# A linear-attention and Mish block on one core: column pieces of the first weights, an interleaved seam between two stages, and two transposes moved

## Chip, core and metric

The kernel runs on one core of a Trainium2 chip. The metric is the device time of one execution in microseconds (us).

The engines are called as the profile calls them: PE is TensorE's matmuls, PEld its weight loads, DVE is VectorE, ACT is ScalarE, POOL is GpSimd, SP issues transfers. Each operation passes through one helper line of the source (L62), so rows are told apart by their tiles, not by their line.

Some words that come back: a *bank* is one of the eight PSUM buffers into which the program lets its matmuls write; to *evacuate* a bank is to copy it out with DVE or ACT, after which it can be used again. A *group* is the eight matmuls that add up in one bank. `rstd` is the factor of a layer norm, which POOL computes; `xr` is the copy of x that is loaded a second time for the residual sum; `KVZ` holds the products kv and z. The *granted clock* is the share of full speed that the profile records for TensorE.

## The reference, cut to what matters

```python
x = A_x                                     # 1 x 2048 x 1024, bf16
h  = x + A(layernorm(x), wqkv, wo)          # linear attention, 32 heads of 32
h2 = h + B(layernorm(h), w1, b1, w2)        # F = 3584

# A: phi(t) = where(t > 0, t + 1, exp(t)) + 1e-6
kv  = sum over s of phi(k) v ;  z = sum over s of phi(k)
o   = phi(q) kv / (phi(q) z + 1e-6) ;  A = o @ wo
# B: u = x @ w1 + b1 ;  act = u * tanh(softplus(u)) ;  B = act @ w2
```

The rows are handled in 16 tiles of 128. TensorE is busy for 668.4 us of the span, the next engine, ACT, for 338.8, so what can be won is TensorE's idle time, and its time at a reduced clock.

## The kernel before: the parts concerned

The program is written as five queues of operations, one for each engine, with explicit semaphore waits; an engine executes its queue in order (in the trace of before, an ACT copy whose input is ready at 326.40 us starts at 340.31, when the ACT work queued ahead of it is done). `ins` adds an operation and returns a token, `wait` makes the queue wait for one.

*The start.* The K and V columns of wqkv arrive in four pieces by rows. The first group of eight matmuls (k = 0 to 7) accumulates over all 1024 rows, so it needs all four pieces:

```python
T_b1 = sp.dma(b1row[:, :], b1_v, d_b1)
T_wkv = [pool.dma(wqkv_sb[:, 2*i:2*i+2, D:3*D], wqkv_v[:, 2*i:2*i+2, D:3*D], d_wkv[i]) for i in range(4)]
T_wq = pool.dma(...) ; T_wo = pool.dma(...)
# b1: a PE transpose and a DVE copy, first in both queues        (cut)
for t in range(NT):
    ...                                       # transposes(t + 1), LN1_prep(t + 2)
    for j in range(4):
        for k in range(KT):
            if t == 0 and j == 0 and k % 2 == 0:
                pe.wait(T_wkv[k // 2])
            tk = pe.ins("matmul", bank[:, :], lhsT=xnT[:, k, ...], rhs=wqkv_sb[:, k, D + j*512: ...], ...)
    if t % 4 == 3:                            # after every fourth tile: 8 groups of Q, on two PSUM banks
        ...
```

*The seam.* After the last Q block come eight groups of KV products, each copied out of PSUM by eight small DVE copies, and only then the first attention tile:

```python
for g in range(NG):
    ...                                       # 16 matmuls into bank g % 4
    for j in range(4):
        dve.ins("tensor_copy", KVZ[rs, g, 32*j:32*(j+1)], bank[rs, 32*j:32*(j+1)], mark=False)
        tkz = dve.ins("tensor_copy", KVZ[rs, g, 128+j:129+j], bank[rs, 128:129])
def stage_A(t):
    pe.wait(T_KVZ[NG - 1])
    ...
for i in range(NT + 1):                       # A: numerator, denominator; B: transpose; C: wo, residual; D: transpose
    stage_A(i); stage_B(i - 1); stage_C(i - 2); stage_D(i - 3)          # bounds of i cut
```

*The tail of that loop.* The transposes of the last two tiles (D) stand behind the first chunk of the second half. Both write the same PSUM bank, and the second waits for the ACT copy of the first:

```python
def stage_D(t):
    pe.wait(T_hn[t])
    if t >= 1:
        pe.wait(T_hnT[t - 1])                 # the one bank must be empty
    tb = tpview(hn_bank)
    ...                                       # 8 transposes
    act.wait(tk_)
    T_hnT[t] = act.ins("activation", hnT[...], tb[:, :, :], ACT.Copy)

H_chunk(0)                                    # layernorm(h) @ w1 for 256 rows; on ACT: Exp, Ln, Tanh in batches
stage_D(NT - 2)
stage_D(NT - 1)
H_chunk(1)
I_chunk(0)                                    # act @ w2
```

Of the kernel before, what the change touches and what calls it, by code (L numbers as in the profile page):

```python
# [20 lines left out]
class _Q:  # L21
# [24 lines left out]
            self.waited[tok.key] = tok.val  # L46
            self.ops.append(("w", tok.sem, tok.val))

    def dma(self, out, in_, dsem, inc=16, **kwargs):
        dsem.total += inc  # L50
        self.ops.append(("d", out, in_, dsem.sem, inc, kwargs))
        return _Tok(dsem.sem, dsem.total, dsem.key)

    def emit(self, block):
        ops = self.ops

        def section(eng):
            for op in ops:
                k = op[0]
                if k == "i":  # L60
                    _, method, args, kwargs, sem = op
                    i = getattr(eng, method)(*args, **kwargs)  # L62
                    if sem is not None:
                        i.then_inc(sem, 1)
                elif k == "w":
                    eng.wait_ge(op[1], op[2])
                else:
                    _, out, in_, sem, inc, kwargs = op
                    eng.dma_start(out, in_, **kwargs).then_inc(sem, inc)

        getattr(block, self.kind)(section)

# [11 lines left out]
def bass_sequential_preLN__linear_attn_block__dense_activation_mish__prompt_kernel(  # L84
# [4 lines left out]
    NT = S // 128  # L89
# [105 lines left out]
    T_x = {}  # L195
    for t in range(min(NXS, NT)):
        T_x[t] = sp.dma(xs[:, t % NXS, :], x_t[t], d_x[t % NXS])
    T_b1 = sp.dma(b1row[:, :], b1_v, d_b1)
    T_wkv = [pool.dma(wqkv_sb[:, 2 * i:2 * i + 2, D:3 * D], wqkv_v[:, 2 * i:2 * i + 2, D:3 * D], d_wkv[i])
             for i in range(4)]  # L200
    T_wq = pool.dma(wqkv_sb[:, :, 0:D], wqkv_v[:, :, 0:D], d_wq)
    T_wo = pool.dma(wo_sb[:, :, :], wo_v, d_wo)

    pe.wait(T_ident, T_b1)
    t_b1 = pe.ins("transpose", tpview(banks[0])[:, 0, 0:FT], b1row[:, :], ident[0:FT, 0:FT])
    dve.wait(t_b1)
    T_b1col = dve.ins("tensor_copy", b1col[:, :], tpview(banks[0])[:, 0, 0:FT])

    T_tp = {}
    T_tpev = {}  # L210
# [41 lines left out]

    def transposes(u):
        tb = tpview(banks[u % 2])
        pe.wait(T_norm[u])
        if u == 0:
            pe.wait(T_b1col)
        if u >= 2:
            pe.wait(T_tpev[u - 2])
        for k in range(KT):  # L260
# [6 lines left out]
    q_banks = [banks[6], banks[7]]  # L267
    q_use = [0]
    T_qbank_free = [None, None]

    LN1_prep(0)
    if NT > 1:
        LN1_prep(1)
    transposes(0)

    for t in range(NT):
        if t + 1 < NT:
            transposes(t + 1)
        if t + 2 < NT:
            LN1_prep(t + 2)  # L280
        pe.wait(T_tpev[t])
        for j in range(4):
            bank = kv_banks[j]
            if t >= 1:
                pe.wait(T_kvev[(t - 1, j)])
            for k in range(KT):
                if t == 0 and j == 0 and k % 2 == 0:
                    pe.wait(T_wkv[k // 2])
                tk = pe.ins("matmul", bank[:, :], lhsT=xnT[:, k, t * 128:(t + 1) * 128],
                            rhs=wqkv_sb[:, k, D + j * 512:D + (j + 1) * 512], start=(k == 0), stop=(k == KT - 1),  # L290
                            mark=(k == KT - 1))
            if j < 2:
                act.wait(tk)
                dve.wait(tk)
                td = phi_evac(bank, pk[:, t, j * 512:(j + 1) * 512])
                T_kvev[(t, j)] = td
                T_pk[t] = td
            else:
                act.wait(tk)
                gs = 4 * (j - 2)  # L300
                T_kvev[(t, j)] = act.ins("activation", v_ext[:, t, gs:gs + 4, 0:128],
                                         bank[:, :].rearrange("p (g c) -> p g c", g=4), ACT.Copy)
                T_v[t] = T_kvev[(t, j)]
        if t % 4 == 3:
            c = t // 4
            pe.wait(T_wq)
            for g in range(NG):
                qb = q_use[0] % 2
                q_use[0] += 1
                bank = q_banks[qb]  # L310
                pe.wait(T_qbank_free[qb])
                for k in range(KT):
                    tk = pe.ins("matmul", bank[:, :], lhsT=wqkv_sb[:, k, g * 128:(g + 1) * 128],
                                rhs=xnT[:, k, c * 512:(c + 1) * 512], start=(k == 0), stop=(k == KT - 1),
                                mark=(k == KT - 1))
                act.wait(tk)
                dve.wait(tk)
                td = phi_evac(bank, pqT[:, g, c * 512:(c + 1) * 512])
                T_qbank_free[qb] = td
                T_qev[(g, c)] = td  # L320

    T_phase1_pe = tk

    if dbg is not None and "pk" in dbg:
        sp.wait(T_pk[NT - 1], T_v[NT - 1], T_qev[(NG - 1, NT // 4 - 1)])
        for t in range(NT):
            sp.dma(dbg["pk"][t], pk[:, t, :], d_dbg)
            sp.dma(dbg["v"][t], v_ext[:, t, :, 0:128], d_dbg)
        for g in range(NG):
            sp.dma(dbg["pqT"][g], pqT[:, g, :], d_dbg)  # L330
        for k in range(KT):
            sp.dma(dbg["xnT"][k], xnT[:, k, :], d_dbg)

    kvb = [banks[2], banks[3], banks[4], banks[5]]
    T_KVZ = {}
    for g in range(NG):
        bank = kvb[g % 4]
        if g < 4:
            pe.wait(T_kvev[(NT - 1, g)])
        else:  # L340
            pe.wait(T_KVZ[g - 4])
        pe.wait(T_pk[NT - 1], T_v[NT - 1])
        for t in range(NT):
            tk = pe.ins("matmul", bank[:, 0:129], lhsT=pk[:, t, g * 128:(g + 1) * 128], rhs=v_ext[:, t, g, 0:129],
                        start=(t == 0), stop=(t == NT - 1), mark=(t == NT - 1))
        dve.wait(tk, T_const)
        for j in range(4):
            rs = slice(32 * j, 32 * (j + 1))
            dve.ins("tensor_copy", KVZ[rs, g, 32 * j:32 * (j + 1)], bank[rs, 32 * j:32 * (j + 1)], mark=False)
            tkz = dve.ins("tensor_copy", KVZ[rs, g, 128 + j:129 + j], bank[rs, 128:129])  # L350
        T_KVZ[g] = tkz

    if dbg is not None and "KVZ" in dbg:
        sp.wait(T_KVZ[NG - 1])
        sp.dma(dbg["KVZ"], KVZ[:, :, :], d_dbg)

    act.wait(T_phase1_pe, T_tpev[NT - 1], T_norm[NT - 1])
    T_w1 = [act.dma(w1_sb[:, 4 * i:4 * i + 4, :], w1_v[:, 4 * i:4 * i + 4, :], d_w1[i]) for i in range(2)]

    if stop_after == "phase2":  # L360
        _finish(nc, sp, act, pe, dve, pool, [d_dbg] if dbg is not None else [])
        return

    att_banks = [banks[4], banks[5], banks[6]]
    otp_bank = banks[7]
    h_banks = [banks[0], banks[1]]
    hn_bank = banks[2]
    T_attev = {}
    T_oT = {}
    T_otp = {}  # L370
# [5 lines left out]
    T_xr = {}  # L376
    T_hstore = {}

    sp.wait(T_KVZ[NG - 1])
    for t in range(3):  # L380
        T_xr[t] = sp.dma(xr[:, t % 3, :], x_t[t], d_xr[t % 3])

    def stage_A(t):
        ob = t % 2
# [47 lines left out]
    def stage_C(t):  # L432
        ob = t % 2
        hs = t % 3
        pe.wait(T_oT[t], T_wo, T_xr[t])
        if t >= 1:
            pe.wait(T_hev[t - 1])
        htok = []
# [33 lines left out]
        T_hn[t] = dve.ins("tensor_scalar", hn[:, ob, :], hst[:, hs, :], mv[:, r, 0:1], rstd[:, r:r + 1],  # L472
                          op0=ALU.subtract, op1=ALU.mult)

    def stage_D(t):
        ob = t % 2
        pe.wait(T_hn[t])
        if t >= 1:
            pe.wait(T_hnT[t - 1])
        tb = tpview(hn_bank)  # L480
        for k in range(KT):
            tk_ = pe.ins("transpose", tb[:, k, :], hn[:, ob, k * 128:(k + 1) * 128], ident[:, :], mark=(k == KT - 1))
        T_hntp[t] = tk_
        act.wait(tk_)
        T_hnT[t] = act.ins("activation", hnT[:, t // 2, :, (t % 2) * 128:(t % 2) * 128 + 128], tb[:, :, :], ACT.Copy)

    for i in range(NT + 1):
        if i < NT:
            stage_A(i)
        if 0 <= i - 1 < NT:  # L490
            stage_B(i - 1)
        if 0 <= i - 2 < NT:
            stage_C(i - 2)
        if 0 <= i - 3 < NT:
            stage_D(i - 3)
# [40 lines left out]

    pool.wait(d_hst[0].tok(), d_hst[1].tok(), d_hst[2].tok())
    sp.wait(T_hev[NT - 1])
    dve.wait(T_wol[NT - 1])

    def H_chunk(c):
        ab = c % 2
        MBPc = MBP_list[c]
        pe.wait(T_w1[0], T_w1[1], T_b1col, T_attev[NT - 1])
        pe.wait(T_hnT[2 * c], T_hnT[2 * c + 1])
        if c >= 2:
            pe.wait(T_f2done[c - 2])
# [4 lines left out]
        while p0 < NPR:  # L552
# [3 lines left out]
            for p in batch:  # L556
                ent = hb_fifo.pop(0)
                prent[p] = ent
                for e_ in range(2):
# [13 lines left out]
                                 op0=ALU.add)  # L573
                    T_f1free[fb] = th
                hbtok[p] = th
            wks = {}
            te = {}
            for p in batch:
# [10 lines left out]
            for p in batch:  # L589
                act.wait(tl[p])  # L590
                tt[p] = act.ins("activation", wk_ring[:, wks[p], :, :], wk_ring[:, wks[p], :, :], ACT.Tanh)
            for p in batch:
                pool.wait(tt[p], hbtok[p])
                if c >= 2:
# [50 lines left out]
            sp.wait(tko)  # L645
            T_ost[t] = sp.dma(out_t[t], ost[:, t % 2, :], d_ost[t % 2])

    H_chunk(0)
    if not tail_D_done[0]:
        stage_D(NT - 2)  # L650
        stage_D(NT - 1)
    H_chunk(1)
    I_chunk(0)
    for c in range(2, NCH):
# [42 lines left out]
```

## Time and profile before

| | before |
|---|---|
| time, median of the first 5 runs | 715.23 us (714.94 to 717.22) |
| span of the profiled run | 713.6 us |
| PE busy | 668.4 us (94%) |
| mean granted TensorE clock | 0.978 |

A page of a profile is read from the top down: busy shares first, then the span in 40 slices, then the waits. Two more lines of the windows view give the measure that the change is held to. Columns: stretch, length, busy time (and instructions) of PE, PEld, DVE, ACT and POOL, granted clock, share of the DMA engines, GB/s.

```profile
180.20:217.34 37.14, 29.68 (x242) 18.18 (x241) 23.76 (x101) 7.42 (x11) 0.00 (x0) 0.86 0.55 219
299.70:393.09 93.39, 76.88 (x578) 56.92 (x576) 31.15 (x65) 61.53 (x97) 31.89 (x29) 0.91 0.26 91
```

The first runs from the last Q block to the second half of the first output projection, the second from chunk 0 to chunk 2 of the second half. PE is idle for 7.5 us in the one and 16.5 us in the other, at a granted clock of 0.86 and 0.91.

### The profile page before, as it was taken

The numbers are of one execution on the slowest core, as the hardware profiler recorded it, in microseconds if no ns is written. First come the engines' busy times: TensorE is split into PE (matmuls) and PEld (weight loads), VectorE is DVE, ScalarE is ACT, GpSimd is POOL, SyncE is SP. The second block draws the span as 40 slices with busy tenths as digits, with TensorE's granted clock in tenths as the row PEclk, the third lists the DMA queues.
The fourth block names the chain that finished last, engine by engine and source line by source line (L and its number), as shares of the span: only waits on it lengthen the run. The fifth ranks groups of instructions, "written<-read, shape, count | busy, mean of one in ns | idle before, by whom it ended". The sixth has DMA issues, their size and how long they took to land.

```text
span 713.6 us, 10800 instructions
## 1 busy us (share of the span) xinstructions
PE 668.4 (94%) x4385; PEld 404.5 (57%) x4385; DVE 319.1 (45%) x737; ACT 338.8 (47%) x533; POOL 150.0 (21%) x162
## 2 busy tenths in 40 slices
PE   2999999999969999992899999999999999999998
PEld 1444434444455555582774865856847748658443
DVE  4556647564486788651331522513514315225111
ACT  0233333333304555469493592681862934916800
POOL 4000000000000100106144062061350440531600
PEclk9999999999979999997799999999999999999999
DMA  8610101100093322290000001001001010010001
GB/s 308 252 30 16 31 15 30 31 1 0 1 401 118 117 89 89 87 382 20 1 16 30 30 1 60 1 28 32 2 30 30 2 29 30 1 60 1 31 30 44
DMA packets 18428, 44.74 MB, mean 63 GB/s; under 512 B 1482, under 2 KB 1482, under 8 KB 18378
## 3 DMA queue, kind: packets, MB, share of 16 engines
q1 hardware_dynamic: 11562, 20.98, 9.2%
q10 hardware_dynamic: 4672, 14.68, 5.4%
q0 software_dynamic: 2144, 8.39, 3.1%
q8 instruction: 34, 0.56, 0.3%
q14 instruction: 16, 0.13, 0.1%
HBM read 35.66 MB, written 8.39 MB: 62 GB/s over the span
## 4 chain that ended last, share of the span: by engine, by line
PE 81%; DVE 9%; ACT 6%; DMA 2%; POOL 1%; issue 1%; DVEq 0%; POOLq 0%
PE bank L62 81%; ACT wk_ring L62 3%; DMA wqkv_sb<-in_A_wqkv_dram 2%; DVE o_sb L62 2%; DVE stats L62 1%; DVE pqT L62 1%; DVE KVZ L62 1%; ACT e_ring L62 1%; ACT L62 1%; ACT hst L62 1%; DVE e_ring L62 1%; POOL rstd L62 1%; DVE den_sb L62 1%; DVE hn L62 1%; DVE rden L62 0%
## 5 line engine op out<-in xcount | busy, mean ns | idle before, releaser
L62 PE MATMUL bank<-hnT,w_sb 128*128 128x256 bf16 x1792 | 199.2, 274 | 1.8 <-DVE hb_ring L62 1.5
L62 PE MATMUL bank<-w_sb,actT 128*128 128x512 bf16 x896 | 194.5, 379 | 0.0
L62 PEld LDWEIGHTS bank<-hnT,w_sb 128*128 128x128 bf16 x1792 | 175.8, 98 | 26.4 <-PE bank L62 3.3
L62 PEld LDWEIGHTS bank<-w_sb,actT 128*128 128x128 bf16 x896 | 87.6, 98 | 104.3
L62 ACT ACTIVATE wk_ring<-wk_ring 128x512 bf16<-128x512 bf16 x224 | 120.3, 616 | 0.4
L62 PE MATMUL bank<-wqkv_sb,xnT 128*128 128x512 bf16 x512 | 115.9, 386 | 2.6 <-DMA wqkv_sb<-in_A_wqkv_dram 2.6
L62 POOL TENSOR_TENSOR actT<-hnT,wk_ring 128x512 bf16<-128x512 bf16 x64 | 71.8, 1155 | 214.7 <-ACT wk_ring L62 214.7
L62 DVE TENSOR_TENSOR ost<-bank,hld 128x512 bf16<-128x512 f32 x32 | 22.1, 691 | 172.7 <-PE bank L62 172.7
L62 ACT ACTIVATE wk_ring<-hnT 128x512 bf16<-128x512 bf16 x64 | 38.0, 623 | 119.5 <-DVE hnT L62 119.5
L62 DVE TENSOR_SCALAR hnT<-bank,b1col 128x256 bf16<-128x256 f32 x128 | 61.9, 484 | 68.5 <-PE bank L62 68.5
L62 ACT ACTIVATE e_ring<-bank 128x512 bf16<-128x512 f32 x64 | 38.2, 597 | 100.3 <-PE bank L62 100.3
L62 PEld LDWEIGHTS bank<-wqkv_sb,xnT 128*128 128x128 bf16 x512 | 50.0, 99 | 62.0 <-DMA wqkv_sb<-in_A_wqkv_dram 4.0
L62 POOL TENSOR_TENSOR rstd<-vpe,ccol 128x1 f32<-128x1 f32 x32 | 17.6, 550 | 277.2 <-DVE vpe L62 277.2
L62 PE MATMUL bank<-wo_sb,oT 128*128 128x512 bf16 x256 | 61.7, 385 | 0.3 <-ACT hst L62 0.3
L62 PE MATMUL bank<-xnT,wqkv_sb 128*128 128x512 bf16 x256 | 58.0, 380 | 2.2 <-DVE pqT L62 0.6
L62 POOL TENSOR_TENSOR actT<-hb_ring,wk_ring 128x512 bf16<-128x512 bf16 x40 | 45.0, 1157 | 35.5 <-ACT wk_ring L62 35.5
L62 DVE TENSOR_SCALAR hb_ring<-bank,b1col 128x256 bf16<-128x256 f32 x80 | 38.5, 483 | 30.0 <-PE bank L62 30.0
L62 ACT ACT_TABLE_LOAD x37 | 47.5, 1283 | 1.4 <-PEq L682 0.7
L62 PEld LDWEIGHTS bank<-xnT,wqkv_sb 128*128 128x128 bf16 x256 | 23.1, 98 | 36.4 <-DVE pqT L62 11.6
L62 DVE TENSOR_SCALAR e_ring<-e_ring,ccol 128x512 bf16<-128x512 bf16 x64 | 22.4, 351 | 47.6 <-ACT e_ring L62 47.6
L62 PEld LDWEIGHTS bank<-wo_sb,oT 128*128 128x128 bf16 x256 | 24.6, 99 | 27.9 <-issue 1.6
L62 ACT ACTIVATE hst<-bank 128x512 bf16<-128x512 f32 x32 | 19.1, 597 | 37.5 <-PE bank L62 32.5
(49 smaller groups left out, 384.0 us busy)
## 6 DMA issues: line engine op xcount, KB each, us to landing
w_sb<-in_B_w_dram ACTq DMA_DIRECT2D x4, 3584.0 KB, 18.7
xs<-in_A_x_dram SPq DMA_DIRECT2D x16, 256.0 KB, 2.7
wqkv_sb<-in_A_wqkv_dram POOLq DMA_DIRECT2D x4, 1024.0 KB, 8.7
xr<-in_A_x_dram SPq DMA_DIRECT2D x16, 256.0 KB, 2.8
out_dram<-hst SPq DMA_DIRECT2D x16, 256.0 KB, 2.0
hld<-out_dram SPq DMA_DIRECT2D x16, 256.0 KB, 2.8
out_dram<-ost SPq DMA_DIRECT2D x16, 256.0 KB, 2.0
wqkv_sb<-in_A_wqkv_dram POOLq DMA_DIRECT2D x1, 2048.0 KB, 17.4
```

Of the source, the lines that this page charges most:

```text
L62: i = getattr(eng, method)(*args, **kwargs)
```

## The change

Its intent is to close three holes in TensorE's row: the wait for the first weights, the wait for the KV copies, and the wait for one late ACT copy. The core of the diff, with cuts marked:

```diff
 # 1. start
-    T_b1 = sp.dma(b1row[:, :], b1_v, d_b1)
-    T_wkv = [pool.dma(wqkv_sb[:, 2*i:2*i+2, D:3*D], ..., d_wkv[i]) for i in range(4)]
-    T_wq = pool.dma(...);  T_wo = pool.dma(...)          # and b1's transpose and copy
+    T_wkv = [act.dma(wqkv_sb[:, :, D+512*j:D+512*(j+1)], ..., d_wkv[j]) for j in range(4)]
 ...
+    for t in range(NT):
+        if t == 0:
+            KV_proj(0, [0, 1]);  transposes(1);  LN1_prep(2)
+            T_wq = pool.dma(...)
+            KV_proj(0, [2, 3])
 ...                                                      # wo at t == 2
+        if t == 8:
+            T_b1col = pool.dma(b1col[:, :], B_b1.rearrange("(f p) -> p f", p=128), d_b1, noncontig=...)
 # 2. seam
+            if c < NT // 4 - 1:
+                Q_proj(c, range(NG))
+            else:
+                Q_proj(c, range(0, 2));  phase2_kv(range(0, 4))
+                Q_proj(c, [2]);          phase2_kv(range(4, 6))
+                Q_proj(c, [3]);          phase2_kv(range(6, 8))
+                phase3_xr_init()
+                Q_proj(c, [4, 5]);       stage_A(0)
+                Q_proj(c, [6]);          stage_A(1);  stage_B(0)
+                Q_proj(c, [7])
 ...
-    att_banks = [banks[4], banks[5], banks[6]];  otp_bank = banks[7];  h_banks = [banks[0], banks[1]];  hn_bank = banks[2]
+    att_banks = [banks[2], banks[3], banks[4]];  otp_bank = banks[0];  h_banks = [banks[6], banks[7]];  hn_bank = banks[5]
+    aux_bank = banks[1]
 # 3. tail
-    H_chunk(0)
-    stage_D(NT - 2)
-    stage_D(NT - 1)
+    H_chunk(0, hooks=...)      # behind chunk 0's first batch:
+                               #   PE:  transposes of tile NT-2 into aux_bank and of tile NT-1 into banks[3]
+                               #   ACT: the two copies, behind the first batch's Tanh
```

## The prediction

> **What bounds the kernel now.** I read the page's busy line and slices first, to see whether one engine fills the span and where it does not; then the windows by stage; then the chain and the waits around each hole; last the timeline, for the duration of each instruction that the change moves.
>
> ```profile
> PE 668.4 (94%) x4385; PEld 404.5 (57%) x4385; DVE 319.1 (45%) x737; ACT 338.8 (47%) x533; POOL 150.0 (21%) x162
> PE   2999999999969999992899999999999999999998
> PEclk9999999999979999997799999999999999999999
> ```
>
> TensorE is the bound at 94%, no other engine passes 47%. But three slices of its row are not nines: the first, the twelfth (about 196 to 214 us) and the nineteenth (321 to 339). Beside the last two the granted clock dips as well. So there are three holes, each of which costs its idle time and a slow restart. The windows by stage give their size (columns: stretch, length, busy time of PE, PEld, DVE, ACT, POOL, granted clock, DMA share, GB/s):
>
> ```profile
> 0.00:18.28 18.28, 4.58 (x23) 2.36 (x24) 7.50 (x17) 1.28 (x1) 8.39 (x21) 1.00 0.83 310
> 206.25:217.00 10.75, 7.41 (x48) 5.07 (x49) 7.14 (x21) 2.05 (x2) 0.00 (x0) 0.52 0.97 395
> 331.00:341.40 10.40, 0.03 (x1) 0.04 (x2) 0.00 (x0) 10.24 (x16) 8.13 (x8) 0.50 0.00 0
> 442.00:637.00 195.00, 194.82 (x1344) 131.09 (x1344) 65.14 (x128) 112.66 (x184) 62.57 (x56) 1.00 0.07 23
> ```
>
> The fourth line is the healthy case: between 442 and 637 us TensorE is never idle and nothing can be hidden there. The third is the worst: 10.4 us in which ScalarE works 10.24 us and TensorE 0.03. The waits and the timeline say who holds it at each hole:
>
> ```profile
> PE bank L62 <- ACT hnT L62: 15.0, 1, 15.0
> PE bank L62 <- DVE KVZ L62: 3.6, 1, 3.6
> PE bank L62 <- DMA wqkv_sb<-in_A_wqkv_dram: 2.6, 1, 2.6
> ```
> ```profile
> 18.28 7.47 PE L62 MATMUL bank<-wqkv_sb,xnT 128*128 128x512 bf16 x26 [2.65 <-DMA wqkv_sb<-in_A_wqkv_dram]
> ...
> 26.04 4.26 PE L62 MATMUL bank<-wqkv_sb,xnT 128*128 128x512 bf16 x19
> ...
> 206.25 0.94 PE L62 MATMUL bank<-KVZ,pqT 128*128 128x132 bf16 x8 [3.60 <-DVE KVZ L62]
> ...
> 214.19 3.10 PE L62 MATMUL bank<-wo_sb,oT 128*128 128x512 bf16 x8
> ```
> ```profile
> 341.37 1.04 PE L62 MATMUL bank<-ident,hn 128*128 128x128 bf16 x8 [14.96 <-ACT hnT L62]
> ...
> 342.20 26.66 PE L62 MATMUL bank<-hnT,w_sb 128*128 128x256 bf16 x224
> ```
>
> The bracket is the idle time before a row and what ended it. First, the K/V projection waits until the last of four weight pieces has landed (18.28 us), because its first group reads all 1024 rows. Second, attention waits until VectorE has copied all KVZ blocks out of PSUM. Third, the transposes of the last row tile wait 14.96 us for a ScalarE copy of the tile before it, which stands in ScalarE's program behind the whole activation work of chunk 0.
>
> **What the Trainium skill says.** "TensorE: Matmul & The Clock Gate", section "Part 1: The HAM clock gate", says that an idle TensorE falls to half clock and needs about 3.4 us of work to come back. The trace agrees: granted clock 0.52 and 0.50 in two windows above; the eight matmuls at 214.19 start 0.427 us apart against 0.214 in steady state; the 224 matmuls at 342.20 take 26.5 us to the next stage against 24.4 later. The same page, "Architectural detail", says that ScalarE and VectorE are strict first-in first-out queues and that TensorE's matmuls stay in program order. The third hole is that: a 1.0 us copy holds TensorE for 15 us. "DMA: Bandwidth & Descriptors", section "Issuing engines are not separate DMA queues", says that loads from any engine share the same 16 engines, so moving the weight load from GpSimd to ScalarE buys no bandwidth; the trace can't show that yet, but it shows 381 to 422 GB/s between 8 and 28 us, a filled pipe. Its section "Rules for kernel authors" says that a strided last dimension becomes one descriptor per element; that concerns the new load of b1, and no run here shows it yet.
>
> **The change part by part.**
>
> *The start.* Removed: the b1 row's transpose and its copy (VectorE's first instruction waited for them until 4.67 us), and the weight loads from GpSimd's program, where they held the first rstd until 8.15 us. Changed: four pieces by columns instead of rows, issued first thing by ScalarE, so the first group needs one piece, not four. Rows become 1 KB instead of 4 KB. An estimate of the rate: 4 KB rows ran at 417 GB/s (12 to 14 us), which is 157 ns each on one of 16 engines; 2 KB rows ran at about 387 GB/s (22 to 28 us), 84.7 ns. That is 12 ns fixed and 36 ns per KB, so 48 ns for 1 KB: 340 GB/s. With bytes flowing from about 2.3 us and the x tiles between them, I put the pieces at about 7.5, 10.6, 14.3 and 18 us. Tile 0: x lands near 4.2, normalisation takes 3.0 us (16.29 to 19.28 in the trace for tile 2), transposes and copy 1.8: first K/V group at 9.2, cold (3.4 us) to 12.6, second to 15.1, transposes of tile 1 to 15.7, third to 17.4, fourth from 18 to 19.8. The next transposes need tile 2, whose normalisation follows the second group's evacuation and tile 1's copy on VectorE: 17.8 plus 3.0, so 20.8. Tile 1's projection then starts at 21.4 against 26.04: **4.6 us** gained.
>
> *Last Q block, KV products, first attention tiles.* Before, eight Q groups (180.2 to 195.0), then 128 KV matmuls (7.67 us) and 64 copies on VectorE (9.31 us), then A(0), A(1), B(0), A(2), B(1), and C(0) at 214.19. After, they are interleaved. I laid the order out by hand with a Q group at 1.73 us of TensorE, 0.9 us to VectorE's start and 1.08 us of VectorE; a KV group at 0.96 and 1.16; an attention tile at 0.62 and 2.3. From the same start of 180.2: KV groups 0 to 3 end at 187.5, Q2 189.2, groups 4 and 5 191.2, Q3 192.9, groups 6 and 7 194.8, Q4 and Q5 198.3, with the last KVZ copy at 197.3, before A(0) needs it. A(1) waits for A(0)'s division behind Q5's evacuation, about 2 us idle until 202.6; Q7 ends at 205.5, A(2) and B(1) at 207.2, and C(0) starts at 207.6, when Q7's bank is evacuated. That is 6.6 us earlier, and its first eight matmuls run warm (1.7 of 3.4 us saved), less 0.5 for small gaps I can't place: **7.8 us**.
>
> *Last two transposes moved into chunk 0.* The first activation batch ends at 322.2 in the trace; the two copies (2 x 1.0 us) go there, so ScalarE ends chunk 0 2 us later, at 342.4, and the last product of chunk 0 near 344. TensorE goes from chunk 0 straight into chunk 1: the 14.96 us fall away, with 2.1 of slow restart and 0.3 in the slow transposes: **17.3 us**. Is a new wait waiting behind it? In the old time frame chunk 1 ends near 351.3, after the products of chunk 0, so the second matrix product need not wait. Chunk 2 starts at 375.6, after ScalarE's 27.6 us for chunk 1 (342.4 to 370) and GpSimd's products (near 374). It fits, by one to two microseconds at the tightest.
>
> *Costs.* Chunk 0 reuses banks of the last tile and now waits for its evacuation, 0.9 us later. But three groups in it stopped anyway for VectorE (1.48 us idle before 303.95), so TensorE resumes at the same moment: 0. The w1 load starts some 11 us later, and still has 90 us. GpSimd's b1 load lies beside tile 8, with a tile of slack.
>
> Sum: 4.6 + 7.8 + 17.3 = 29.7 us; 715.2 - 29.7 = 685.5, given as **686**.
>
> **The rivals.** *The b1 load stalls GpSimd.* 3584 two-byte elements are 3584 descriptors. If building them holds GpSimd over about 8 us, the rstd of tile 11 is late, VectorE stands before it, and bank evacuation with it: 5 to 12 us lost, time 691 to 698. For it: the element count. Against: GpSimd's issues of 256 and of 1024 rows both took 0.7 to 0.9 us, hardly more for four times the rows. *Small rows slow the first load.* At 250 GB/s the fourth piece lands near 22.5 us and the start gains about 1.5: time 689. For it: no 1 KB load in this trace. Against: the trend from 4 to 2 KB. *The holes move.* Chunk 2 waits for GpSimd's products, or the 2 us hole at A(1) grows and the clock drops: 2 to 6 us back, 688 to 692. For it: the small margin before chunk 2, and VectorE, which in the interleaved stretch has some 22 us of work in 27. Against: TensorE's period of 48.8 us from chunk 2 on leaves ScalarE ample time.
>
> **Range and chances.** Each rival takes some microseconds; all three together leave about 703. Being better by more than 6 us would need the start to run at full weight rate and A(1) not to wait. So 8 in 10: 680 to 695. Faster by over 2% means under 701: 0.96; within 2%: 0.03; slower: 0.01.
>
> **What would show it.** In the profile after: no wait of PE on ACT hnT near 15 us, and the clock at 0.9 or more in the slice near 310; C(0) 11 to 14 us earlier than 214.19 (start and middle together); tile 1's projection near 21; chunk 2's start some 30 us before 393.09; period 48.8 unchanged after. The prediction is wrong if a new wait above 3 us stands before chunk 2 or the first product of w2, if rstd waits for the b1 load near tile 11, or if the fourth weight piece lands after 21 us.

## The result, and the profile after

The changed kernel takes 684.56 us (median of 8 runs, 684.21 to 685.06) against 715.23 us for the kernel before (median of 15 runs). The ratio is 0.9572, with a 95% interval of 0.9563 to 0.9582. Ratios in this document are the mean time of one kernel's runs over the mean of the other's in the same set of runs, so they are not quite the ratio of the medians quoted.

The head of the page of the changed kernel, to be set beside the three lines in the prediction:

```profile
PE 662.0 (97%) x4384; PEld 401.0 (59%) x4384; DVE 319.0 (47%) x736; ACT 337.9 (49%) x533; POOL 149.0 (22%) x159
PE   5999999999989999999999999999999999999998
PEclk9999999999999999999999999999999999999999
```

The 2 of the nineteenth slice and the 8 behind it are gone, the 6 of the seam has become an 8 (at about 188 to 205 us), the first slice went from 2 to 5, and the clock row has no dip. The mean granted clock is 1.0 instead of 0.978. That row doesn't tell everything: in the changed kernel's window from 8.68 to 15.02 us it gives 1.00, yet the 16 matmuls there start about 0.40 us apart, against 0.216 later. The slow start of the program is seen in the lengths of the rows, not in the recorded clock. PE's busy time itself fell by 6.4 us, with one matmul fewer: matmuls at half clock count as busy for longer.

The windows view of the changed kernel, with the borders at the same places of the program as in the lines of before:

```profile
175.19:203.75 28.56, 25.80 (x243) 16.51 (x242) 22.58 (x101) 7.42 (x11) 0.00 (x0) 1.00 0.18 60
287.60:362.55 74.95, 74.31 (x576) 55.54 (x577) 31.05 (x65) 60.05 (x96) 31.87 (x29) 1.00 0.32 113
362.55:607.00 244.45, 244.14 (x1682) 164.05 (x1683) 81.69 (x161) 143.51 (x232) 78.23 (x70) 1.00 0.07 22
```

The seam went from 37.14 to 28.56 us and the two chunks (with the first product with w2 behind them) from 93.39 to 74.95; the work in them is the same, to a row or two. In the third line, the long second half, PE is as full as it was.

Six marks in the two timelines say where the time came from. All but the last are starts of the same matmuls in both kernels.

| mark | before, us | after, us | earlier by | won since the mark above |
|---|---|---|---|---|
| tile 1's K/V projection | 26.04 | 21.01 | 5.03 | 5.03 |
| last Q block | 180.20 | 175.19 | 5.01 | 0.0 |
| second half of the first output projection, C(0) | 217.34 | 203.75 | 13.59 | 8.58 |
| chunk 0 resumes after its first three groups | 303.95 | 290.96 | 12.99 | -0.60 |
| chunk 2 | 393.09 | 362.55 | 30.54 | 17.55 |
| end of the span | 713.6 | 683.1 | 30.5 | 0.0 |

The rows of PE that carry this in the changed kernel's timeline (start, length, row; in brackets the idle time before it and what ended it):

```profile
8.68 6.51 PE L62 MATMUL bank<-wqkv_sb,xnT 128*128 128x512 bf16 x16 [0.78 <-DVE xnT L62]
...
17.72 1.90 PE L62 MATMUL bank<-wqkv_sb,xnT 128*128 128x512 bf16 x8 [0.36 <-DMA wqkv_sb<-in_A_wqkv_dram]
...
21.01 7.07 PE L62 MATMUL bank<-wqkv_sb,xnT 128*128 128x512 bf16 x32
...
197.03 0.63 PE L62 MATMUL bank<-KVZ,pqT 128*128 128x132 bf16 x8 [1.88 <-DVE o_sb L62]
...
298.83 1.06 PE L62 MATMUL bank<-ident,hn 128*128 128x128 bf16 x16
...
299.73 38.59 PE L62 MATMUL bank<-hnT,w_sb 128*128 128x256 bf16 x352
```

The first group starts at 8.68, long before the fourth weight piece, which is awaited at 17.72. At 197.03 the second attention tile waits 1.88 us for the division of the first: that is most of what is left of the seam's hole (2.76 us idle in all). The 16 transposes at 298.83 are those of the last two tiles, now with no wait in front, and the 352 matmuls behind them (the rest of chunk 0 and all of chunk 1) run without a break.

The waits of PE in the changed kernel (total us, times, longest), for those shown of before:

```profile
PE bank L62 <- DVE o_sb L62: 4.1, 9, 1.9
PE bank L62 <- ACT hst L62: 1.1, 2, 0.8
PE bank L62 <- DMA xr<-in_A_x_dram: 0.4, 1, 0.4
PE bank L62 <- DMA wqkv_sb<-in_A_wqkv_dram: 0.4, 1, 0.4
```

No wait on ACT hnT and none on DVE KVZ is left. Two are new and small: 0.8 us on ACT hst, where chunk 0 now reuses a bank of the last attention tile, and 0.4 us on a reload of x (xr).

### The profile page after: what moved, and what is told of

It is laid out like the page before. It is cut to its first block, busy times and chain, and to the rows that moved or that the text cites. A ratio compares the mean times of both kernels' runs of the same rounds, so it can differ in the third digit from the quotient of the medians. Undisturbed runs are those within 1.5% of the kernel's fastest.

```text
span 683.1 us, 10801 instructions
## 1 busy us (share of the span) xinstructions
PE 662.0 (97%) x4384; PEld 401.0 (59%) x4384; DVE 319.0 (47%) x736; ACT 337.9 (49%) x533; POOL 149.0 (22%) x159
## 4 chain that ended last, share of the span: by engine, by line
PE 87%; DVE 8%; DMA 2%; ACT 2%; issue 1%; POOL 1%; DVEq 0%
PE bank L62 87%; DMA xr<-in_A_x_dram 2%; DVE o_sb L62 2%; DVE stats L62 2%; DVE pqT L62 1%; ACT e_ring L62 1%; ACT hst L62 1%; DVE e_ring L62 1%; POOL rstd L62 1%; DVE den_sb L62 1%; DVE hn L62 0%; DMA xs<-in_A_x_dram 0%; DVE rden L62 0%; DVE vpe L62 0%; DVE mv L62 0%
## 5 line engine op out<-in xcount | busy, mean ns | idle before, releaser
L62 PE MATMUL bank<-hnT,w_sb 128*128 128x256 bf16 x1792 | 197.2, 273 | 1.7 <-ACT hst L62 0.8
L62 DVE TENSOR_SCALAR hb_ring<-bank,b1col 128x256 bf16<-128x256 f32 x80 | 38.5, 483 | 30.9 <-PE bank L62 30.5
```

The costliest lines, as they stand in the source:

```text
L62: i = getattr(eng, method)(*args, **kwargs)
```

## The experiments

Twelve kernels, one of them the changed kernel again, ran in three sets, each set on one chip beside runs of the kernel before (715.03, 715.05 and 715.65 us, medians of 11, 11 and 9). The theory on trial was that of the prediction: three independent holes, each closed by its own part. The rivals were that the parts overlap, that another half of a part does the work, and that the slow stretch after a hole is no matter of the clock. `tail_warm`, `start_only` and `mid_only` change the time by less than 2%; their intervals don't reach 1, and each is read below with its trace. All outputs are right.

### The tail alone, and its two halves

The tail does two things at once: it gives the two transposes different banks, and it moves copies forward in ACT's queue. Three kernels built on the kernel before take these apart. All of them split `stage_D` into its PE part and its ACT part.

`tail_only`, both halves:

```diff
-    H_chunk(0)
-    stage_D(NT - 2)
-    stage_D(NT - 1)
+    def _tail_pe():
+        stage_D_pe(NT - 2, bank=banks[7], wait_prev=False)
+        stage_D_pe(NT - 1, bank=banks[3], wait_prev=False)
+    def _tail_act():
+        stage_D_act(NT - 2, bank=banks[7])
+        stage_D_act(NT - 1, bank=banks[3])
+    H_chunk(0, hooks={"pe": _tail_pe, "act": _tail_act})
```

> The kernel before with only the third part of the change: the transposes of the last two row tiles go into chunk 0 after its first batch, into two different free PSUM banks (7 and 3), and their two ScalarE copies go behind the first batch's tanh. Theory (the three parts are independent and add up; between chunk 0's start and chunk 2's start the changed kernel's trace is 17.55 us shorter): 697.7 us, chunk 2 starts about 375.5, no wait of PE on ACT hnT. Rival (the parts overlap, so that the tail alone is worth less, because ScalarE or GpSimd then hold chunk 1 or 2): 700 to 708.

`tail_banks`, the banks alone, everything left in its place:

```diff
     H_chunk(0)
-    stage_D(NT - 2)
-    stage_D(NT - 1)
+    stage_D_pe(NT - 2, bank=banks[7], wait_prev=False);  stage_D_act(NT - 2, bank=banks[7])
+    stage_D_pe(NT - 1, bank=banks[3], wait_prev=False);  stage_D_act(NT - 1, bank=banks[3])
```

> The kernel before, with the last two transposes left where they are, at the end of chunk 0, and the two ScalarE copies left behind chunk 0's activations; only the two transposes now write two different PSUM banks, so that the second need not wait for the copy of the first. Theory (what holds TensorE is the shared bank; nothing needs the late copies before the first product with w2): 697.7 us, as the full tail change. Rival (the copies' place in ScalarE's order is what costs, the banks alone do not help): 713 to 716.

`tail_order`, the order alone, one shared bank:

```diff
-    H_chunk(0)
-    stage_D(NT - 2)
+    H_chunk(0, hooks={"pe": lambda: stage_D_pe(NT - 2), "act": lambda: stage_D_act(NT - 2)})
     stage_D(NT - 1)
```

> The kernel before, one shared bank for both transposes as it was, but the first of them and its ScalarE copy moved into chunk 0 behind the first batch; the second stays at the end of chunk 0. Theory (either half of the change removes the wait, because the copy is then done near 323 us, before the second transposes at about 327): 697.7 us. Rival (separate banks are needed): 713 to 716.

| run | median, us | ratio to before, 95% | from chunk 0's resumption to chunk 2 in the trace, us |
|---|---|---|---|
| before (first trace) | 715.23 | | 303.95 to 393.09: 89.14 |
| tail_only | 697.66 | 0.9762 (0.9745 to 0.9779) | 303.68 to 375.27: 71.59 |
| tail_banks | 699.06 | 0.9774 (0.9758 to 0.9791) | 305.14 to 376.73: 71.59 |
| tail_order | 698.55 | 0.9769 (0.9752 to 0.9785) | 303.40 to 374.99: 71.59 |
| changed kernel | 684.56 | 0.9572 (0.9563 to 0.9582) | 290.96 to 362.55: 71.59 |

All three shorten the stretch by 17.55 us, the same as the whole change, to the hundredth of a microsecond. The medians differ by up to 1.4 us, but their intervals overlap, and the traces put the differences ahead of that stretch (the resumption itself moves between 303.40 and 305.14, and tile 1's K/V projection, at the very start, already starts at 27.07 in `tail_banks` against 25.69 in `tail_order`, with the same code up to there). So the theory holds, the tail is independent of the rest, and either half is enough: the wait existed only because one bank was shared **and** its copy stood late. The PE rows of `tail_banks` show it with the ACT copies where they were:

```profile
326.99 1.06 PE L62 MATMUL bank<-ident,hn 128*128 128x128 bf16 x16
327.88 24.62 PE L62 MATMUL bank<-hnT,w_sb 128*128 128x256 bf16 x224
352.33 24.34 PE L62 MATMUL bank<-w_sb,actT 128*128 128x512 bf16 x112
```

Both sets of transposes run together and chunk 1 follows at once; the first product with w2 at 352.33 does not wait for the late copies.

### How much of the tail is clock: keep the hole, keep PE busy

`tail_warm` leaves the wait of the kernel before in place and fills it with work of no use:

```diff
     H_chunk(0)
     stage_D(NT - 2)
+    for _ in range(64):
+        pe.ins("matmul", banks[3][:, :], lhsT=w1_sb[:, 0, 0:128], rhs=w1_sb[:, 0, 0:512],
+               start=True, stop=True, mark=False)
     stage_D(NT - 1)
```

> The kernel before with its hole kept, but 64 unused matmuls of 512 columns (13.7 us at 0.214 each) into an idle bank put into it, so that TensorE is busy while it waits. Theory (of the 17.3 us, 2.4 are a restart at half clock, not waiting): the 224 matmuls of chunk 1 take 24.4 to 24.6 us to the next stage instead of 26.5, time 712.8. Rival (the long chunk 1 after the hole has another cause, such as bank evacuation or the activation queue): 715.2, unchanged.

Measured: 713.23 us, ratio 0.9976 (0.9961 to 0.9991), so 0.6 to 2.8 us faster than before. Its PE rows:

```profile
326.87 13.98 PE L62 MATMUL bank<-w_sb 128*128 128x512 bf16 x64
342.00 0.62 PE L62 MATMUL bank<-ident,hn 128*128 128x128 bf16 x8 [1.16 <-ACT hnT L62]
342.46 24.62 PE L62 MATMUL bank<-hnT,w_sb 128*128 128x256 bf16 x224
366.91 24.34 PE L62 MATMUL bank<-w_sb,actT 128*128 128x512 bf16 x112
```

The transposes still wait for the same ACT copy, but the 224 matmuls of chunk 1 now take 24.45 us to the next stage (342.46 to 366.91) instead of 26.49, and from chunk 0's resumption to chunk 2 the trace counts 86.73 us (304.58 to 391.31) instead of 89.14: 2.41 us less, where 2.4 was expected. The profile's granted clock from 341.4 to 368 us is 1.00, where it was 0.91 before. The rival is out: the slow stretch was the restart at half clock. The useless matmuls have no place in a real kernel here, as removing the wait wins both.

### The start alone, and its two halves

`start_only` puts the first part of the diff above into the kernel before (and nothing else of it).

> The kernel before with only the first part of the change: K and V weights in four column pieces issued by ScalarE, the order of tile 0's groups, the q and output weights loaded later, b1 loaded by a strided transfer. Theory (parts add up; in the two traces tile 1's projection starts 5.03 us apart): 710.2 us. Rival (the earlier start is given back later in the first phase, by VectorE or by the later q weights): 712 to 715.

Measured: 710.35 us, ratio 0.9936 (0.9916 to 0.9955). Tile 1's projection starts at 21.08 in its trace. The expected 710.2 is met; the rival's 712 to 715 lies just outside the interval (3.2 to 6.0 us of gain, 709.0 to 711.8 us).

`after_rows` takes the changed kernel and gives it row pieces again, still issued by ACT:

```diff
-    T_wkv = [act.dma(wqkv_sb[:, :, D+512*j:D+512*(j+1)], wqkv_v[:, :, D+512*j:D+512*(j+1)], d_wkv[j]) for j in range(4)]
+    T_wkv = [act.dma(wqkv_sb[:, 2*i:2*i+2, D:3*D], wqkv_v[:, 2*i:2*i+2, D:3*D], d_wkv[i]) for i in range(4)]
 ...
-            if t == 0:
-                pe.wait(T_wkv[j])
+                if t == 0 and j == 0 and k % 2 == 0:
+                    pe.wait(T_wkv[k // 2])
```

> The changed kernel, with the K and V weights in four pieces by rows again (4 KB rows, the first group needs all four), still issued by ScalarE at the start. Theory (the shape of the pieces is what pays): 4.7 MB at 0.417 MB per us from 2.3 us land near 14.6, tile 1's projection starts near 23.7 instead of 21.0, time 687.3. Rival (issuing early from ScalarE and freeing VectorE and GpSimd is what pays): 684.6, unchanged.

Measured: 689.53 us, ratio to before 0.9646 (0.9625 to 0.9667), so 5.0 us slower than the changed kernel. The direction is the theory's, the size is not: 2.7 us were expected. PE's rows:

```profile
8.44 2.07 PE L62 MATMUL bank<-wqkv_sb,xnT 128*128 128x512 bf16 x4 [0.79 <-DVE xnT L62]
12.87 1.04 PE L62 MATMUL bank<-wqkv_sb,xnT 128*128 128x512 bf16 x2 [2.36 <-DMA wqkv_sb<-in_A_wqkv_dram]
15.27 4.45 PE L62 MATMUL bank<-wqkv_sb,xnT 128*128 128x512 bf16 x10 [1.36 <-DMA wqkv_sb<-in_A_wqkv_dram]
...
25.76 4.48 PE L62 MATMUL bank<-wqkv_sb,xnT 128*128 128x512 bf16 x20
```

The last piece arrives near 15.2, where 14.6 was worked out. What was not worked out is the rest of the delay: behind the waits at 12.87 and 15.27 the next ten matmuls still take 4.45 us, so they run at half speed, and two groups end only with the transposes at 19.51, against 15.02 in the changed kernel. The normalisation of tile 2 slides behind them (its rstd is at 23.89 instead of 19.37). That the waits are what kept PE slow is the likely reading; no run shows it apart. Tile 1's projection starts at 25.76, almost where it stood before the change (26.04). So the shape of the pieces is worth practically all of the start's gain (25.76 less 21.01 is 4.75 us of 5.03, and 5.0 in the times), and with row pieces issuing early by ACT is worth only about 0.3 us. These marks scatter: in the traces with the old start tile 1's projection starts between 25.69 and 27.45, in those with the new one between 20.36 and 21.18.

`after_gpsimd` keeps the columns and gives the issue back to POOL (`act.dma` becomes `pool.dma` in that one line).

> The changed kernel, with the four column pieces issued by GpSimd again instead of ScalarE. Theory (the issuer matters less than the shape, but GpSimd can only issue after its own set-up at 3.3 us and then delays the first rstd): tile 1's projection starts near 22.3, time 685.9. Rival (rows of 1 KB are slow in the ring of GpSimd): later than 24, time over 688.

Measured: 685.96 us, ratio 0.9592 (0.9571 to 0.9613). Tile 1's projection starts at 22.34. Both as expected: POOL issues from 3.33 to 7.04 us, the first rstd waits until 7.05 instead of 5.67, and 1.3 us are lost. So with column pieces the issuer is worth 1.3 us. The rate of the transfer is the same from either: in windows of 2 us, both traces move 347 to 359 GB/s while the 1 KB rows are under way (from 8 to 16 us).

### The seam alone

`mid_only` is the kernel before with the interleaving and the new banks; start and tail are undone, the last two transposes sharing bank 1.

> The kernel before with only the second part: the last Q block interleaved with the KV products and the first attention tiles, with the PSUM banks that this needs; start and tail as before (both last transposes share one bank again, bank 1). Theory: the traces show 8.58 us by the second half of C(0), of which 0.6 are lost again in the attention loop, where the w1 load now lies beside the reloads of x: 707.2 us. Rival (the middle's gain came partly from the other parts, or its bank move costs at chunk 0): 709 to 713.

Measured: 706.40 us, ratio 0.9884 (0.9862 to 0.9905). From the last Q block to the second half of C(0) its trace counts 28.55 us (181.39 to 209.94), the changed kernel's 28.56, before 37.14. The wait of 15.0 us on ACT hnT is still there. The theory (707.2 us) holds; the rival's 709 to 713 lies outside the interval (705.2 to 708.3 us). The seam was not taken apart further: no run separates the interleaved KV products from the early attention tiles or from the new banks.

The three parts alone win 17.37, 4.70 and 8.65 us, by the medians of their own sets: 30.72 together. The whole change wins 715.23 - 684.56 = 30.67. They add up. Each of the three is known only to about 1.3 us either way, so that the two totals agree to 0.05 us is luck.

### Where 0.6 us went, and a version that beats both

In the attention loop the changed kernel lost 0.60 us of what it had won, and the prediction had not seen that. One reload of x, 256 KB, was long under way beside the load of w1 (7.3 MB). The two lay beside each other before as well: there w1 was issued at 195.19 us, ahead of the first three reloads (206.22), which took 7.8 to 11.5 us, and PE waited for none (in the trace of `start_only` it waited 0.48 for the first). Now w1 is issued at 199.88, behind those three (191.84), and meets a reload issued at 211.72 that PE soon needs. The chain view of the changed kernel has it (start, length, what):

```profile
211.72 12.36 DMA xr<-in_A_x_dram
```

PE's row behind it, in the timeline:

```profile
224.13 1.90 PE L62 MATMUL bank<-wo_sb,oT 128*128 128x512 bf16 x8 [0.44 <-DMA xr<-in_A_x_dram]
```

The median reload takes 3.0 us. Three further kernels follow this up and use what the seam taught; a fourth is the changed kernel itself, to have it on the same chip.

> The changed kernel itself, unedited, on the same chip as the three below, to compare with: 684.6 us.

Measured: 684.37 us (684.19 to 684.58), as before.

`q_spread` treats the first three Q blocks as the seam treated the fourth:

```diff
+        if t >= 4:
+            Q_proj(t // 4 - 1, [2 * (t % 4), 2 * (t % 4) + 1])
 ...
         if t % 4 == 3:
             c = t // 4
-            if c < NT // 4 - 1:
-                Q_proj(c, range(NG))
-            else:
+            if c == NT // 4 - 1:
```

> The changed kernel, with the first three Q blocks (eight groups on two PSUM banks in a row) also spread: two groups after each of the next four tiles' K/V projection. In the changed kernel's trace each such block loses 3 waits of TensorE on DVE pqT of about 0.3 us (period of two groups 3.78 us against 3.46 of matmul). Theory (the same cure as in the middle part, the evacuation hidden behind other banks' matmuls): 2.9 us less, 681.7. Rival (the Q evacuations then collide with K/V evacuations on VectorE and the waits move there): 684 to 685.

Measured: 681.39 us (681.04 to 681.55); 2.98 us less than the changed kernel on the same chip, whose runs do not overlap with these. The trace has the gain ahead of the loop: from tile 1's projection to the second half of C(0) it counts 179.72 us (20.36 to 200.08) instead of 182.74 (21.01 to 203.75). The waits for evacuated Q banks stand mostly with the weight loads: PEld waits on DVE pqT for 1.0 us in 2 waits instead of 8.7 in 17, PE itself for 0.2 instead of 0.6.

`q_spread_w1` also cuts the load of w1:

```diff
-    T_w1 = [act.dma(w1_sb[:, 4*i:4*i+4, :], w1_v[:, 4*i:4*i+4, :], d_w1[i]) for i in range(2)]
 ...
     for i in range(2, NT + 1):
+        if i - 2 < KT:
+            T_w1.append(act.dma(w1_sb[:, i - 2, :], w1_v[:, i - 2, :], d_w1[i - 2]))
```

> As q_spread, and the load of w1, 7.3 MB issued at once when the last Q group ends, is cut into eight pieces, one issued in each of eight attention tiles. Theory (in the changed kernel the attention loop lost 0.6 us against before, because one reload of x lay 12.4 us in the queue beside w1, and a wait of PE on DMA xr of 0.44 us followed): that wait is gone, 681.1. Rival (the 0.6 us has another cause, such as the new banks): 681.7, as q_spread.

Measured: 681.05 us (680.76 to 681.41). The gain over `q_spread`, 0.34 us, is too small for the spread of the runs. The trace decides: from the second half of C(0) to chunk 0's resumption it counts 86.62 us (200.90 to 287.52), with `q_spread` 87.42 (200.08 to 287.50), with the changed kernel 87.21, and before 86.61. The whole loss is gone and with it the wait on xr. The other kernels with the new seam agree: the stretch is 87.00 us with a wait on xr of 0.22 (`after_rows`), 87.11 with 0.31 (`after_again`), 87.21 with 0.44, 87.42 with 0.63 (`q_spread`), and 86.62 with none, here and in `combined`. In the time of this profiled run (681.41, the slowest of the four) nothing shows, because it reached C(0) 0.8 us later. The landing times of the x reloads issued from 190 us on (issue to landing, us) in `q_spread`, then in `q_spread_w1`:

```profile
DMA to landing us min/median/max: 2.6/2.8/12.6
```
```profile
DMA to landing us min/median/max: 2.6/4.6/7.1
```

The typical reload is slower beside the pieces, but none is slow enough to be waited for. What counts is the longest one against the three tiles of prefetch.

`combined` also changes the start:

```diff
     dve.wait(T_const)
     act.wait(T_const)
+    act.ins("activation", ccol[:, 4:5], ccol[:, 0:1], ACT.Exp, mark=False)      # table load early
+    pe.wait(T_ident)
+    for _ in range(34):                                                         # clock up before the data
+        pe.ins("matmul", banks[7][:, 0:128], lhsT=ident[:, :], rhs=ident[:, :], start=True, stop=True, mark=False)
 ...
         if t == 0:
-            KV_proj(0, [0, 1]);  transposes(1);  LN1_prep(2);  T_wq = ...;  KV_proj(0, [2, 3])
+            KV_proj(0, [0, 1]);  transposes(1);  LN1_prep(2);  KV_proj(1, [0]);  KV_proj(0, [2]);  T_wq = ...
+            KV_proj(1, [1]);  KV_proj(0, [3]);  transposes(2);  LN1_prep(3);  KV_proj(1, [2, 3])
```

> As q_spread_w1, with a changed start: 34 unused matmuls on the identity from about 3.2 us, so that TensorE is at full clock when the first data arrive; one throw-away Exp, so that the table load lies before the data; and tiles 0 and 1 interleaved, so that the third and fourth weight pieces are needed later. Theory: tile 1's projection ends near 24.3 instead of 27.9, about 3 us less, 678. Rival (the start is bound by the arrival of x and of the pieces, so only the 0.4 and 0.9 us waits can be taken): 680.

Measured: 679.52 us (679.28 to 681.06), the fastest of all, 0.9499 of before (0.9475 to 0.9523) and by the medians 4.85 us under the changed kernel on the same chip. But the step over `q_spread_w1` is 1.5 us, not 3, and nearer to the rival's 680; one of the four runs (681.06) is no faster than `q_spread_w1`. PE's rows of the start:

```profile
3.16 3.75 PE L62 MATMUL bank<-ident 128*128 128x128 bf16 x34 [3.16 <-POOL ident L62]
6.95 0.62 PE L62 MATMUL bank<-ident,xn 128*128 128x128 bf16 x8
8.36 1.90 PE L62 MATMUL bank<-wqkv_sb,xnT 128*128 128x512 bf16 x8 [0.79 <-DVE xnT L62]
...
14.90 7.08 PE L62 MATMUL bank<-wqkv_sb,xnT 128*128 128x512 bf16 x32 [2.03 <-DVE xnT L62]
```

The warm-up works: the first two groups take 1.90 us each, as later ones do, where the changed kernel's first two took 6.51 together. The time is lost again at 14.90, where PE waits 2.03 us for tile 1's transposed copy, which stands on DVE behind the evacuation of two K groups. Neither the theory nor the rival named that wait; it is an order on DVE, not the arrival of data. Moving that copy forward was not tried.

## Why the prediction was right, point by point

The time was predicted at 686 and measured at 684.56. The sum of the parts was 29.7 us and the traces show 30.5. The signs it named came true: C(0) starts 12.38 us earlier, tile 1's projection at 21.01, chunk 2 30.54 us earlier, and the period stays 48.86 us. That the sum is so close is partly luck: the three parts won 1.46 us more than was said and an unseen cost took 0.60 back, and the start's mark alone scatters by 0.8 us (new start) to 1.8 us (old) between traces. (Of the slices, the twentieth and the last are below nine too; they belong to the third hole and to the end.)

- **The start** was put at 4.6 us and is 5.03. Its steps hold closely: the rate of 1 KB rows was estimated at 340 GB/s and is 347 to 359 (the 417 GB/s behind it came from a stretch in which a third of the packets were not weight rows); the fourth piece was put at 18 and is awaited until 17.72; the next transposes were put after 20.8 and start at 20.55, held by tile 2's normalisation, as said. The strength of this part was also put in the right place, the pieces' shape: `after_rows` shows it.
- **The seam** was put at 7.8 us and is 8.58. The wait at the second attention tile was given as about 2 us and is 1.88; from the start of the last Q block to C(0) 27.4 us were worked out and 26.62 measured (175.19 to 201.81). So C(0) starts 7.37 us earlier relative to the Q block, not 6.6, and the 0.5 us that were taken off "for small gaps I can't place" do not exist. The restart was read too large: of the eight matmuls at 214.19 about six start 0.427 us apart, the row is 3.10 us long and not 3.4, and running them warm saves 1.21 us (from C(0) to its second half, 3.15 to 1.94), not 1.7.
- **The tail** was put at 17.3 us and is 17.55, made up as said: 15 of waiting, 2.4 of restart (`tail_warm`). The question of whether a new wait stands behind it was answered rightly, and the times were met: POOL's last product of chunk 1 ends at 361.5 (it starts the seven at 353.71 and takes 7.81), and chunk 2 starts at 362.55. But this was not a margin, because chunk 2 doesn't wait for that product: by the code and the trace its first eight pairs of sums go into `hnT`, of which POOL read the last part until 344.4, and the first `hb_ring` buffer is written only at 377.61. The nearer margin is the one before the first product with w2, at 338.15, for which chunk 0's last product must be done (331.07). One point was told too broadly. The prediction, like the change, treats bank and order as one cure; the runs show that each alone is one.
- **The costs** were put at zero. The new wait of chunk 0 is: 0.78 us before it, and 0.55 instead of 1.48 behind it, so PE resumes as far behind the last attention tile as it did. "The w1 load starts some 11 us later, and still has 90 us" was near enough for w1 (it is issued 9.7 us later counted from the last Q block, 4.7 on the clock), but the question was put to the wrong transfer. It cost 0.6 us through the reloads of x beside it, as `q_spread_w1` shows.
- **The rivals.** The strided load of b1 held POOL for 1.80 us (its row at 106.87) and landed in 5.7; the queue shows 3600 packets for it, and it stalls nothing. Small rows were a little slower, not at 250 GB/s. The holes did not move, apart from those 0.6 us.

## What to carry to other kernels

Look in TensorE's row for single long waits before looking for many short ones, and ask of each what two conditions make it: here a shared PSUM bank and a late place in another engine's in-order queue, either of which could be dropped. Cut the first weights along the dimension that the first group does not sum over, even if rows become shorter. When a large load is moved, check the small periodic loads that it will now lie beside, and give them smaller neighbours.

## What the Trainium skill lacked or had wrong

- "DMA: Bandwidth & Descriptors", section "Specifications", gives 512 B as the least transfer for the full rate, and the page has no rates for this chip with rows of 1 or 2 KB. Here, in windows of 2 us, loads with rows of 4 KB moved at 403 to 426 GB/s (issued by POOL and, in `after_rows`, by ACT), with rows of 2 KB at 381 to 389 (POOL), and with rows of 1 KB at 347 to 359 (ACT and POOL alike); x tiles with rows of 2 KB are mixed in.
- The same page, section "Queues, rings and completion order", says that each DMA engine takes turns between queues by packets, from which one would expect a small transfer to pass a large one quickly. Here the slowest load of 256 KB beside 7.3 MB issued from another queue took 11.5 us in the kernel before and 12.2 to 12.6 in those with the new seam, against 2.7 alone; why is not shown. The page has no figure for that case.
- The same page has no time for issuing a strided transfer from GpSimd. Here 3584 two-byte elements held POOL for 1.80 us, against 0.89 to 1.11 for 1024 rows of 2 KB.
- "TensorE: Matmul & The Clock Gate", section "Part 1: The HAM clock gate", by which about 3.4 us of sustained work bring full clock, was borne out: in `combined` 3.75 us of matmuls on the identity brought the clock up before the data, and in `tail_warm` keeping TensorE busy through the hole of 15 us saved the 2.4 us of restart.
